# Four more chunk pairs of the FFNs in Strassen's form, a third set of partial-sum copies, and new written-out orders, in a four-layer linear-attention and SwiGLU kernel on one core

## The chip, the cores and the metric

The kernel runs on one core of one Trainium2 chip. The metric is the device time of one execution in microseconds. TensorE is called PE, VectorE DVE, ScalarE ACT, GpSimd POOL, and SyncE SP (here it only issues DMAs); PEld is PE's loading of weights.

## The reference

Four layers work on x, 2048 tokens by 512, in bfloat16. Layers 0 and 2 are linear attention, layers 1 and 3 are SwiGLU FFNs, each behind a layer norm and with a residual:

```python
def _A_ref(x, wqkv, wo):      # 32 heads of 16
    phi = lambda t: jnp.where(t > 0, t + 1, jnp.exp(t)) + 1e-6
    ...
    kv = jnp.einsum("bhsd,bhse->bhde", pk, v)
    num = jnp.einsum("bhqd,bhde->bhqe", pq, kv)
    ...
    return (o, heads side by side) @ wo
def _B_ref(x, w_gate, w_up, w_down):   # 512 -> 1792 -> 512
    return (_silu(x @ w_gate) * (x @ w_up)) @ w_down
x = x + _A_ref(_layernorm(x), ...)
x = x + _B_ref(_layernorm(x), ...)
x = x + _A_ref(_layernorm(x), ...)
x = x + _B_ref(_layernorm(x), ...)
```

## The kernel before, in words

Everything stays in SBUF. The 2048 tokens are 16 tiles of 128 (`T`), in 4 groups of 512 (`G`). The hidden width 1792 is 14 chunks of 128 (`NF`), taken as 7 pairs of chunks j and j+7 (`NK`).

**The order of the work is written out.** PE follows the list `PROGRAM`, one token per piece of work. A token is a layer, a letter and indices: `2k3` projects the keys of tile 3 in layer 2, `q` the queries, `g` adds a tile to the products of keys and normed rows, `v` and `m` make the four blocks of M (the merged key-value and output matrix, kept in `GT`), `w` multiplies a tile of queries by M and adds the residual, `u` is one gate-and-up chunk, `y` one Strassen product, `p` one Strassen product of the down projection. The other four engines follow the lists in `ORDER`, one name per instruction, as `1u104.h`. The program derives the semaphores from what each instruction reads and writes; an engine works through its list in order and waits at its head. PSUM has 8 banks; `bank()` gives the one whose last use stands longest ago in `PROGRAM`, so a matmul can wait for whoever reads that bank's last contents.

**A plain pair** (`gu`) is two `u` tokens: 16 matmuls of 512 columns (line 483, the one line of all matmuls but the transposes). For each chunk ACT takes the silu of the gate (L954, name `.silu`) and DVE multiplies by the up part (L959, `.h`). In layer 1, once layer 2 has begun, the silu is made of a tanh (`.tanh`, L942) and one more DVE pass (`.gst`).

**A Strassen pair** (`gs`) makes the same two chunks with 7 products instead of 8, each for gate and up at once: tokens `y` g j 1 to 7, 4 matmuls of 256 columns each, 28 in all. It needs sums of weight blocks (`gs_piece`, L1040, `.ws`), made for two pairs at a time, and of blocks of the transposed rows (`gs_rows`, L1086, four `.xs` per group of tokens). Products 1, 6, 7 and 4 add up in one PSUM bank, 5 and 3 in another, 2 has its own. After products 1, 6 and 7 ACT copies the running sum to SBUF (L1179, `.cp`). DVE adds such a copy to another bank (L1158, `.ca`) three times; ACT takes the silu of half of it (L1150, `.sih`, four times, once straight from PSUM); the gate-up product is one 256-column multiplication on POOL or DVE (L1173, `.hp`, three times) and one on DVE (L1189, `.hh`). The copies live in lent buffers (`gs_copies`): a set of three per pair in work. Two sets exist in layer 1, so two pairs can be open at once; layer 3 has a third set (`fam_slot`). 22 of the 56 pairs are in Strassen's form: three in layer 1 (group 1, j = 2, 0, 1) and 19 in layer 3.

**The down projection** (`down`, tokens `p`) is in Strassen's form everywhere, 14 matmuls of 256 columns per product. It needs sums of the hidden blocks (`sums_of_h`, L1251, `.sb` and `.sa`) and of blocks of w_down (`load_down`, L579, `Wd.tw`).

When the last Strassen pair that uses `Wo` as its home for row sums is through, `Wo` is read again from memory (`reload`, name `R.ldo`, a DMA that POOL issues, line 526). In `wo` (L905 to 912) the four matmuls of a tile take the blocks c = 0, 1, 2, 3 of M in this order, whatever order the `m` tokens have (`2m1 2m0 2m3 2m2` in layer 2, `0m0 0m2 0m1 0m3` in layer 0); `evac` (L786 on ACT, L789 on DVE) copies each block from PSUM to `GT`. `scale` (L882, `.pqn`) multiplies queries by 1/den and must come before the `w` of that tile.

Of the kernel before, what the change touches and what calls it, by code (L numbers as in the profile page):

```python
# [224 lines left out]
0q10.id1 0d0.rex2 i.c1 0q20.exp 0d1.ln 0d1.rex1 0d1.rex3 0G2.evac 0G3.evac 0q30.exp 0d1.rex2 0d1.rex 0q31.exp 0M0.evac
0M1.evac 0M3.evac 0q33.exp 0d2.ln 0d2.rxs 0q33.id1 1x1.sq 1x2.sq 1x3.sq 1x2.apply 1x0.sq 1x3.apply 0q32.exp 1x5.sq
1x6.sq 1x4.sq 1x11.sq 1u012.silu 1u001.silu 1x7.sq 1u007.silu 1x9.sq 1x4.apply 0d3.rep 1u000.silu 1u011.silu
1u006.silu 1u004.silu 0d3.rep1 1x7.apply 0d3.rep2 1u005.silu 1x6.apply 1u013.silu 1x10.sq 1u003.silu 1x8.sq 1u002.silu
0d3.rep3 1u010.silu 1u008.silu 1y121.cp 1x9.apply 1u113.silu 1u110.silu 1u009.silu 1u104.silu 1y101.cp 1y126.cp
# [1279 lines left out]
```

## Time and profile before

| what | value |
|---|---|
| median of 3 runs | 405.15 us (404.96 to 405.56) |
| profiled execution, its own time | 405.13 us |
| its span | 403.4 us |
| instructions | 7572 |
| PE, PEld, DVE, ACT, POOL busy | 397.1, 252.0, 331.8, 254.6, 176.8 us |
| granted clock of PE | 1.00 over the span |
| DMA | 23.84 MB, 59 GB/s mean |

The span runs from the first to the last instruction of the profile; some 1.7 us of the time lie around it. A PE matmul's bar in the profile is longer than the distance to the next one, as matmuls overlap; the distance between starts is what a matmul costs in a stream.

### The profile page before, as it was taken

The numbers are of one execution on the slowest core, as the hardware profiler recorded it, in microseconds if no ns is written. First come the engines' busy times: TensorE is split into PE (matmuls) and PEld (weight loads), VectorE is DVE, ScalarE is ACT, GpSimd is POOL, SyncE is SP. The second block draws the span as 40 slices with busy tenths as digits, with TensorE's granted clock in tenths as the row PEclk, the third lists the DMA queues.
The fourth block names the chain that finished last, engine by engine and source line by source line (L and its number), as shares of the span: only waits on it lengthen the run. The fifth ranks groups of instructions, "written<-read, shape, count | busy, mean of one in ns | idle before, by whom it ended". The sixth has DMA issues, their size and how long they took to land.

```text
span 403.4 us, 7572 instructions
## 1 busy us (share of the span) xinstructions
PE 397.1 (98%) x2798; PEld 252.0 (62%) x2798; DVE 331.8 (82%) x786; ACT 254.6 (63%) x525; POOL 176.8 (44%) x304
## 2 busy tenths in 40 slices
PE   7999999999999999999999999999999999999997
PEld 5445544445785764445776444444568788888886
DVE  5996598569986766979998476979889799899997
ACT  5999887483635537445166878686654673786550
POOL 4723335999787400210136603475677141421230
PEclk9999999999999999999999999999999999999999
DMA  8647682732002140010002105333200110100011
GB/s 273 157 80 238 154 160 63 191 72 28 2 13 67 26 80 13 2 39 0 2 16 52 39 3 78 66 54 78 41 13 2 41 53 2 53 2 2 2 52 54
DMA packets 53334, 23.84 MB, mean 59 GB/s; under 512 B 46448, under 2 KB 52080, under 8 KB 53296
## 3 DMA queue, kind: packets, MB, share of 16 engines
q1 hardware_dynamic: 51264, 16.27, 19.4%
q0 software_dynamic: 1488, 6.55, 5.1%
q10 hardware_dynamic: 544, 0.52, 0.4%
q8 instruction: 22, 0.36, 0.4%
q14 instruction: 16, 0.13, 0.1%
HBM read 10.22 MB, written 2.10 MB: 31 GB/s over the span
## 4 chain that ended last, share of the span: by engine, by line
PE 95%; DVE 2%; DMA 1%; issue 0%; SPq 0%; ACT 0%; DVEq 0%
PE pb L483 94%; DMA X<-in_A_x_dram 1%; DVE hT L959 0%; DVE X L912 0%; SPq L526 0%; ACT GT L786 0%; DVE Wd L579 0%; DVE xnB L646 0%; DVE pq L1371 0%; PE pb L670 0%; DVE pq L882 0%; DVE stats L600 0%; DVE xnA L1297 0%; DVE KVT L800 0%; DVEq L1479 0%
## 5 line engine op out<-in xcount | busy, mean ns | idle before, releaser
L483 PE MATMUL pb<-xnT,Wg 128*128 128x512 bf16 (+1 forms) x360 | 86.6, 353 | 0.1
L483 PE MATMUL pb<-xnT,Wu 128*128 128x512 bf16 (+1 forms) x360 | 86.6, 353 | 0.0
L483 PEld LDWEIGHTS pb<-xnT,Wu 128*128 128x128 bf16 x360 | 35.2, 98 | 33.1
L483 PEld LDWEIGHTS pb<-xnT,Wg 128*128 128x128 bf16 x360 | 35.1, 98 | 29.4 <-issue 0.6
L635 POOL TENSOR_TENSOR rstd<-vpe,negh 128x1 f32<-128x1 f32 x62 | 36.8, 595 | 19.3 <-DVE vpe L631 17.6
L959 DVE TENSOR_TENSOR hT<-tht,pb 128x512 bf16<-128x512 f32 x46 | 30.6, 681 | 16.6 <-ACT tht L954 10.2
L1179 ACT ACTIVATE pq<-pb 128x512 f32<-128x512 f32 x48 | 28.1, 595 | 24.4 <-PE pb L483 23.0
L954 ACT ACTIVATE tht<-pb 128x512 f32<-128x512 f32 x46 | 26.5, 591 | 23.4 <-PE pb L483 21.4
L1173 POOL TENSOR_TENSOR hT<-pq 128x256 bf16<-128x256 f32 x30 | 22.6, 762 | 42.3 <-ACT pq L1150 42.0
L483 PE MATMUL pb<-Wd,hT 128*128 128x256 bf16 x336 | 40.3, 273 | 0.0
L691 ACT ACTIVATE etmp<-pb 128x512 bf16<-128x512 f32 x64 | 36.3, 602 | 5.9 <-PE pb L483 3.7
L483 PEld LDWEIGHTS pb<-Wd,hT 128*128 128x128 bf16 x336 | 32.9, 98 | 4.9 <-POOL nmr L639 0.3
L1158 DVE TENSOR_TENSOR pq<-pb,pq 128x512 f32<-128x512 f32 x48 | 31.9, 684 | 4.1 <-PE pb L483 2.2
L483 PE MATMUL pb<-xnT,Wqkv 128*128 128x512 bf16 x128 | 32.2, 379 | 0.0
L696 DVE TENSOR_SCALAR etmp<-etmp 128x512 bf16<-128x512 bf16 x64 | 19.0, 304 | 15.2 <-ACT etmp L691 15.0
L483 PE MATMUL pb<-Wqkv,xnT 128*128 128x512 bf16 x128 | 31.2, 379 | 0.0
L483 PE MATMUL pb<-pk,xnA 128*128 128x512 bf16 x128 | 30.7, 379 | 0.0
L483 PE MATMUL pb<-GT,pq 128*128 128x512 bf16 x128 | 30.0, 379 | 0.4 <-ACT GT L786 0.3
L942 ACT ACTIVATE tht<-pb 128x512 f32<-128x512 f32 x22 | 12.8, 596 | 23.4 <-PE pb L483 20.3
L619 POOL TENSOR_SCALAR mv<-sums 128x1 f32<-128x1 f32 x52 | 13.5, 266 | 31.3 <-DVE sums L1381 22.0
L615 ACT ACTIVATE etmp<-X,sums 128x512 bf16<-128x512 bf16 x32 | 22.9, 717 | 5.7 <-DVE X L912 5.7
L1150 ACT ACTIVATE pq<-pq 128x256 f32<-128x256 f32 x48 | 18.8, 411 | 10.7 <-DVE pq L1158 10.4
(207 smaller groups left out, 837.8 us busy)
## 6 DMA issues: line engine op xcount, KB each, us to landing
out_dram<-pq SPq DMA_DIRECT2D x16, 128.0 KB, 1.8
Wg<-in_B_w_gate_dram POOLq DMA_DIRECT2D x4, 448.0 KB, 5.3
Wu<-in_B_w_up_dram POOLq DMA_DIRECT2D x4, 448.0 KB, 5.5
Wd<-in_B_w_down_dram POOLq DMA_DIRECT2D x7, 256.0 KB, 3.6
...
```

What stands on the lines that cost most here:

```text
L483: return op("pe", lambda e: e.matmul(o_ap, lhsT=lhsT, rhs=rhs, start=start, stop=stop, skip_group_check=skip), r=r, w=w, n=n)
L615: op("act", lambda a: a.activation(out=sq_ap, in_=X[:, t, :], func=ACT.Square, scale=-float(D), bias=sums[:, t:t + 1], accum_out=mv[:, t, ...
L619: op("pool", lambda p: p.tensor_scalar(out=mv[:, t, 0:1], in0=sums[:, t:t + 1], scalar1=-1.0 / D, scalar2=None, op0=ALU.mult), r=[f"sm{t}" ...
L635: op("pool", lambda p: p.tensor_tensor(out=rstd[:, t:t + 1], in0=vpe[:, t:t + 1], in1=negh[:], op=ALU.pow), r=[f"vp{t}", "negh"], w=[f"rs{ ...
L691: exps.append(op("act", lambda a: a.activation(out=etmp[e][:], in_=PB[pb], func=ACT.Exp), r=[f"pb{pb}"], w=[f"e{e}"], after=silus, kind="e ...
L696: op("dve", lambda v: v.tensor_scalar(out=etmp[e][:], in0=etmp[e][:], scalar1=1.0, scalar2=1e-6, op0=ALU.min, op1=ALU.add), r=[f"e{e}"], w ...
L954: silus.append(op("act", lambda e: e.activation(out=tht[a][:], in_=PB[pg], func=ACT.Silu), r=[f"pb{pg}"], w=[f"th{a}"], after=exps, kind=" ...
L959: op("dve", lambda v: v.tensor_tensor(out=hT[h][:, j, :], in0=tht[a][:], in1=PB[pu], op=ALU.mult), r=[f"pb{pu}", f"th{a}"], w=hk, kind="h")
L1150: silus.append(op("act", lambda e: e.activation(out=o_ap, in_=i_ap, func=ACT.Silu), r=r, w=w, after=exps, kind="sih" if len(w) == 1 else " ...
L1158: op("dve", lambda v: v.tensor_tensor(out=c, in0=PB[b], in1=c, op=ALU.add), r=[f"pb{b}", k], w=[k], kind="ca")
L1173: lambda e: e.tensor_tensor(out=hT[h][:, jj, o:o + 256], in0=c[:, 0:256], in1=c[:, 256:512], op=ALU.mult),
L1179: op("act", lambda e: e.activation(out=c, in_=PB[pb], func=ACT.Copy), r=pk_, w=[k], kind="cp")
```

## The change

- Layer 1: the pairs `1y13` (group 1), `1y21` and `1y20` (group 2) go into Strassen's form in place of `1u103 1u110`, `1u201 1u208` and `1u200 1u207`. Layer 3: `3y15` in place of `3u105 3u112`. The weight sums that they need are among those already made; group 2 of layer 1 needs its four row sums (`1gx2`, on POOL).
- Layer 1 gets a third set of copies too, in `GT` and `rrep`.
- Two plain chunks of layer 1, `1u209` and `1u211`, have their up part copied by ACT (`.uc`) and multiplied by POOL (`.hc`) instead of DVE's `.h`.
- `wo` takes the blocks of M in the order in which the `m` tokens stand.
- In the head, DVE makes the statistics of tile 2 (ACT did), and some tiny steps change places between POOL, DVE and ACT; `0g0` moves ahead of `0q03`.
- The lists of all engines are written anew around it. `KVT` becomes a part of `etmp`'s buffer.

```diff
@@ PROGRAM
-1u007 1u000 1u004 1u011 1u006 1u005 1u003 1u013 1u010 1u002 1y121 1u008 1u113 1u009 0w13 1u110 0w14 1y126 1y101 1u104
...
-1y122 1u105 1y106 0w15 1y125 1y102 0w12 1y127 1y107 1p01 1y124 1y123 1y105 1y104 1u112 1y103 1p05 1u103 1p06 1y111
+1u007 1u000 1u004 1u011 1u006 1u005 1u003 1u013 1u010 1u002 1y121 1u008 1u113 1u009 0w13 0w14 1y126 1y101 1u104 1y122
+1u105 1y106 0w15 1y125 1y102 0w12 1y127 1y107 1p01 1y131 1y124 1y132 1y136 1y123 1y105 1y137 1y104 1u112 1y135 1y134
+1y103 1p05 1p06 1y111 1y112 1y115 1p07 1y116 1p02 1y133 1y117 1p04 1p03 1y114 1u111 1y113 1u106 1u213 1u206 1y201 1p11
+1y211 1p15 1y216 1y206 1y212 1y217 1p16 1y215 1u210 1y213 1y214 1y202 1y207 1y205 1p17 1p12 1y204 1y203 1p14 1u203
...
+3y136 3y122 3y127 3y137 3p03 3y151 3y124 3y135 3y152 3y156 3u113 3y157 3y123 3y155 3p04 3y133 3y141 3y154 3y134 3y211
...
@@ ORDER, DVE
-1x11.apply Wd.tw8 1u002.h 1u010.h 0d3.pqn 1u008.h 0d3.pqn1 Wd.tw1 0d3.pqn2 0d3.pqn3 1u113.h 1u009.h 0w13.res 1u110.h
...
+0d3.pqn1 1u005.h 1u013.h 1u010.h 1x11.apply 0d3.pqn2 Wd.tw8 Wd.tw1 1u002.h 0d3.pqn3 1u008.h 0d3.pqn 1u113.h Wd.tw7
...
@@ ORDER, POOL
-1x13.vpe 1y122.hp Wd.tw3 1y123.hp 1y103.hp Wd.tw1 1y127.hp 1x8.pow 1x14.pow 1y105.hp 2x2.negm R.ldo 1x13.pow 1y112.hp
...
+1y122.hp Wd.tw5 1x14.pow 1x12.negm 1y123.hp 1y127.hp 1x14.nmr 1x13.pow 1x8.pow 1x15.vpe 1x13.negm 1x15.negm 1y112.hp
+1y103.hp R.ldo 1y133.hp 1y105.hp 1gx2.xs 1y135.hp 1x13.nmr 1y102.hp 1y117.hp 2x3.negm 1y113.hp 1y132.hp 1gx2.xs2
...
@@ m_mm, wo
+            m_of.setdefault(L, []).append(c)
...
-            for c in range(NC):
-                mm(pb, pq[n][:, c, tl * P:(tl + 1) * P], GT[:, c, :], c == 0, c == NC - 1,
+            for c in m_of[L]:
+                mm(pb, pq[n][:, c, tl * P:(tl + 1) * P], GT[:, c, :], c == m_of[L][0], c == m_of[L][-1],
@@ fam_slot
-            if L == 3 and r.left.get(r.k % 2, 0) > 0 and not third[0]:
+            if r.left.get(r.k % 2, 0) > 0 and not third[0]:
                 third[0] = True
+                if L == 1 and len(gs_tmp[L]) == 6:
...
+                    for x, olds in ((gt[:, 0:1024], ["GT0", "GT1"]), (gt[:, 1024:], ["GT2", "GT3"]), (rreps, ["rrep0", "rrep1"])):
...
                 return 2
```

## Rows read from the trace of the kernel before

**Rows 1.** The page: busy time by engine, and the ending chain's shares by engine

```profile
PE 397.1 (98%) x2798; PEld 252.0 (62%) x2798; DVE 331.8 (82%) x786; ACT 254.6 (63%) x525; POOL 176.8 (44%) x304
...
PE 95%; DVE 2%; DMA 1%; issue 0%; SPq 0%; ACT 0%; DVEq 0%
```

**Rows 2.** Timeline of PE, 101 to 107 us: start, us, what, out<-in, count

```profile
101.03 1.03 PE L483 MATMUL pb<-GT,pq 128*128 128x512 bf16 x4
101.89 0.60 PE L483 MATMUL pb<-Wo,xnA 128*128 128x256 bf16 x4
...
104.50 1.69 PE L483 MATMUL pb<-Wd,hT 128*128 128x256 bf16 x14
106.03 0.38 PE L483 MATMUL pb<-Wo,Wg 128*128 128x256 bf16 x2
```

**Rows 3.** The ending chain in order of time: start, us, what

```profile
91.97 0.35 DVE pq L882
...
262.57 1.94 DVE X L912 x6
```

**Rows 4.** Stretches: PE, PEld, DVE, ACT, POOL busy, clock, DMA

```profile
86.00:104.00 18.00, 17.86 (x99) 9.46 (x98) 17.92 (x29) 7.99 (x15) 17.86 (x19) 1.00 0.18 28
104.00:126.00 22.00, 22.00 (x179) 17.27 (x177) 19.37 (x53) 11.14 (x28) 16.13 (x21) 1.00 0.06 13
...
300.00:330.00 30.00, 30.00 (x262) 25.30 (x260) 26.66 (x53) 18.63 (x42) 14.31 (x19) 1.00 0.13 32
...
360.00:400.00 40.00, 39.95 (x367) 35.23 (x365) 38.89 (x80) 20.32 (x49) 7.87 (x11) 1.00 0.06 18
```

**Rows 5.** The page's costliest groups: busy, mean ns of one, idle before

```profile
L483 PEld LDWEIGHTS pb<-xnT,Wu 128*128 128x128 bf16 x360 | 35.2, 98 | 33.1
...
L959 DVE TENSOR_TENSOR hT<-tht,pb 128x512 bf16<-128x512 f32 x46 | 30.6, 681 | 16.6 <-ACT tht L954 10.2
L1179 ACT ACTIVATE pq<-pb 128x512 f32<-128x512 f32 x48 | 28.1, 595 | 24.4 <-PE pb L483 23.0
...
L1173 POOL TENSOR_TENSOR hT<-pq 128x256 bf16<-128x256 f32 x30 | 22.6, 762 | 42.3 <-ACT pq L1150 42.0
...
L1158 DVE TENSOR_TENSOR pq<-pb,pq 128x512 f32<-128x512 f32 x48 | 31.9, 684 | 4.1 <-PE pb L483 2.2
...
L1150 ACT ACTIVATE pq<-pq 128x256 f32<-128x256 f32 x48 | 18.8, 411 | 10.7 <-DVE pq L1158 10.4
```

**Rows 6.** Groups of instructions on POOL, 86 to 150 us, shapes apart

```profile
L1086 POOL TENSOR_TENSOR Wo<-xnT 128x512 bf16<-128x512 bf16 x2 | 2.5, 1272 | 0.0
```

**Rows 7.** Timeline of PE, 90 to 98 us

```profile
91.20 1.03 PE L483 MATMUL pb<-xnT,Wu 128*128 128x512 bf16 x4
92.37 1.04 PE L483 MATMUL pb<-GT,pq 128*128 128x512 bf16 x4
```

**Rows 8.** Timeline of DVE, 82 to 106 us

```profile
84.93 0.69 DVE L959 TENSOR_TENSOR hT<-tht,pb 128x512 bf16<-128x512 f32 x1 [1.69 <-ACT tht L954]
...
90.08 1.29 DVE L882 TENSOR_TENSOR pq<-pq,RT 128x512 bf16<-128x512 bf16 x1
...
91.90 0.41 DVE L882 TENSOR_TENSOR pq<-pq,RT 128x512 bf16<-128x512 bf16 x1
```

**Rows 9.** Timeline of POOL, 123 to 131 us

```profile
124.78 0.84 POOL L526 DMA_DIRECT2D Wo<-in_A_wo_dram  x1
...
126.19 2.08 POOL L1173 TENSOR_TENSOR hT<-pq 128x256 bf16<-128x256 f32 x3
```

**Rows 10.** Timeline of PE, 122 to 131.5 us

```profile
130.80 0.93 PE L483 MATMUL pb<-Wd,hT 128*128 128x256 bf16 x7
```

**Rows 11.** Timeline of all engines, 250 to 253 us

```profile
250.59 1.57 ACT L786 ACTIVATE GT<-pb 128x512 bf16<-128x512 f32 x3
...
251.81 1.46 PE L483 MATMUL pb<-GT,pq 128*128 128x512 bf16 x6 [0.28 <-ACT GT L786]
```

**Rows 12.** Timeline of all engines, 4 to 10 us

```profile
6.29 0.69 DVE L600 BATCH_NORM_STATS2 stats<-X 128x6 f32<-128x512 bf16 x1 [0.16 <-DMA X<-in_A_x_dram]
```

More of the change, by code (lines that the diff above doesn't have):

```diff
@@ L225 @@
[L225 to L229, printed above, removed]
@@ L267 @@
-0q23.ts 0q23.phi 0z.zm 0q22.ts 0q21.ts 0q10.ts 0q21.phi 0q22.phi 0q10.phi 0d0.pqn1 0q20.ts 0q20.phi 0G0.evac 0G1.evac
-0q30.ts 0v.mask 0v.mask1 0q30.phi 0d0.pqn 0q31.ts 0M2.evac 0q31.phi 0d1.pqn1 0q33.ts 0w1.res 0d2.dT 0w2.res 0q33.phi
-1x1.vpe 0w3.res 1x2.vpe 1x1.apply 0w0.res 0r2.pqn 0d1.pqn 1x3.vpe 0d1.pqn2 0r2.pqn1 0d1.pqn3 0r2.pqn2 1x0.vpe 0r2.pqn3
-0q32.ts 1x0.apply 0w5.res 0q32.phi 0w6.res 0w4.res 0w7.res 0w11.res 0d3.den 1x5.vpe 0w9.res 0w10.res 0w8.res 0d3.rcp
-1x5.apply 1u007.h 1u012.h 1u001.h Wd.tw 1x9.vpe 1x7.vpe 1u011.h 1u000.h 1u006.h 1u004.h 1u005.h 1u003.h Wd.tw6 1u013.h
@@ L292 @@
-2q23.phi 2q22.phi 2d0.pqn1 2G0.evac 2G1.evac 2d0.pqn 2v.mask 2v.mask1 2q33.ts 2d1.dT 2M3.evac 2r1.pqn 2r1.pqn1 2w3.res
-2r1.pqn2 2w2.res 2r1.pqn3 3x3.apply 2q33.phi 2w0.res 3x2.apply 2d2.pqn 2w1.res 2w4.res 2d2.pqn3 2d2.pqn2 3x1.vpe
-2q30.ts 2q30.phi 2d2.pqn1 2q32.ts 3x1.apply 2q32.phi 2w6.res 2w9.res 2w7.res 2w8.res 2w5.res 2w10.res 2d3.den 2d3.rcp
-3W1.ws2 2w11.res 3u001.h 3u004.h 3W1.ws4 3x4.apply 3x7.apply 3W1.ws 3u008.h 3W1.ws1 3u010.h 2d3.pqn 3x9.vpe 3u000.h
-3x9.apply 2w12.res 3W0.ws1 3W1.ws3 3W0.ws 2d3.pqn3 3x11.vpe 3u009.h 3x8.apply 3u005.h 3W2.ws 2d3.pqn1 2d3.pqn2
@@ new lines @@
+0G1.evac 0q30.ts 0v.mask 0v.mask1 0q30.phi 0M2.evac 0q31.ts 0d0.pqn 0q31.phi 0d1.pqn1 0q33.ts 0w1.res 0d2.dT 0w2.res
+0q33.phi 1x1.vpe 0w3.res 1x2.vpe 1x1.apply 0w0.res 0d1.pqn 1x3.vpe 0r2.pqn 0d1.pqn2 0r2.pqn1 0d1.pqn3 0r2.pqn2 1x0.vpe
+0r2.pqn3 0q32.ts 1x0.apply 0w5.res 0q32.phi 0w6.res 0w4.res 0w11.res 0d3.den 0w7.res 0w9.res 0w10.res 0w8.res 1x5.vpe
+1x9.vpe 1x5.apply 0d3.rcp 1u012.h 1u001.h 1u007.h 1u011.h 1x7.vpe 1u000.h 1u004.h 1u006.h Wd.tw 1u003.h Wd.tw6
+0d3.pqn1 1u005.h 1u013.h 1u010.h 1x11.apply 0d3.pqn2 Wd.tw8 Wd.tw1 1u002.h 0d3.pqn3 1u008.h 0d3.pqn 1u113.h Wd.tw7
@@ new lines @@
+2x8.apply 1p33.rh1 1p37.uu 2k11.ts 2k11.phi 1p37.rh 1p37.rh1 1p34.rh 1p34.tot 1p34.rh1 2x14.tot 2x14.vpe 1p32.rh1
+2x12.tot 2x15.vpe 2x14.apply 2q02.ts 1p32.rh 1p32.tot 2q02.phi 2x15.apply 2q00.ts 2q00.phi 2q12.ts 2q12.phi 2x12.apply
+2k9.ts 2k9.phi 2k10.ts 2k10.phi 2k8.ts 2k14.ts 2k8.phi 2k14.phi 2k15.ts 2k15.phi 2q11.ts 2k14.zs 2k13.ts 2k13.phi
+2k12.ts 2q11.phi 2k12.phi 2k13.zs 2q31.ts 2k12.zs 2q31.phi 2q21.ts 2s.zh 2s.zl 2q20.ts 2q20.phi 2z.zm 2q03.ts 2q03.phi
+2q21.phi 2q13.ts 2q23.ts 2q13.phi 2d0.pqn 2q22.ts 2q23.phi 2q22.phi 2d0.pqn1 2G0.evac 2G1.evac 2v.mask 2v.mask1
@@ new lines @@
+2q33.ts 2d1.dT 2M3.evac 2r1.pqn 2r1.pqn1 2w3.res 2r1.pqn2 2w2.res 2r1.pqn3 3x3.apply 2q33.phi 2w0.res 3x2.apply
+2d2.pqn 2w1.res 2q30.ts 2q32.ts 2q30.phi 2d2.pqn3 3x1.vpe 2d2.pqn2 2w4.res 2d2.pqn1 3x1.apply 2q32.phi 2w6.res 2w8.res
+3W1.ws2 3W1.ws4 2w9.res 2d3.den 2w7.res 2w5.res 2w10.res 3W1.ws 2w11.res 2d3.rcp 3u001.h 3W2.ws 3u008.h 3x7.apply
+3x4.apply 3W1.ws3 3W1.ws1 3x9.vpe 2d3.pqn 3u004.h 3W0.ws1 3u010.h 2d3.pqn1 3x11.vpe 3u000.h 3x9.apply 3W0.ws 2d3.pqn3
+2w12.res 3u005.h 3u009.h 3x8.apply 3u012.h 2d3.pqn2 2w15.res 3u002.h 3W0.ws2 3u011.h 3gx1.xs 2w14.res 2w13.res
@@ L314 @@
+3p35.uu 3p36.uu 3h3.sa3 3p36.uu1 3p32.rh1 3p33.rh 3p33.rh1 3p37.uu 3p37.rh 3p34.rh 3p37.rh1 3p34.rh1
 """,
     "pool": """
[L316 to L319 removed]
@@ new lines @@
+0x15.vpe 0x13.pow 0x14.nmr 0x15.pow i.c3 0x8.pow 0x12.vpe 0x12.pow i.ld i.ld3 i.ld2 i.ld1 i.ld4 i.ld8 0d0.pqn1 i.ld6
+i.ld7 i.ld5 0d0.pqn 1x1.negm 1x2.negm 1x1.pow 1x2.pow 1x2.nmr 1x3.pow 1x3.negm 1x0.negm 1x3.nmr 1x0.pow 1x4.negm
+1x6.negm 1x7.negm 1x4.vpe 1x5.negm Wd.ld2 1x4.pow 1x6.vpe 1x6.pow 1x5.pow 1x11.negm 1x6.nmr Wd.ld 1x4.nmr Wd.ld1
+1x11.vpe 1W0.ws4 1x9.pow Wd.ld4 1W0.ws6 1W1.ws Wd.ld5 1x7.pow 1x11.pow 1x7.nmr Wd.ld3 Wd.ld6 1W1.ws1 1W0.ws5 1W1.ws2
+1x9.negm 1W0.ws 1W1.ws4 1x9.nmr 1W1.ws5 1x8.negm 1W1.ws6 Wd.tw6 1gx1.xs 1x10.vpe 1x10.pow 1gx1.xs1 1W1.ws7 1W0.ws1
@@ L933, in gu @@
             hk = [f"h{h}_{j}a", f"h{h}_{j}b"]
-            uc = rreps[:, 0:1024].bitcast(FP32) if L == 1 and f"1c{g}{j:02d}" in ON_ACT else None
+            late = f"{L}c{g}{j:02d}" in ON_ACT and ("rrep0" not in pr.lent if L == 1 else all(f"2w{t}" in given for t in range(T)))
+            uc, uk = (rreps[:, 0:1024].bitcast(FP32), ["rrep0", "rrep1"]) if L == 1 else (etmps[:, 1024:2048].bitcast(FP32), ["uc"])
+            if late and L == 3 and "uc" not in pr.bufs:
+                lend(L, "uc", ["e2", "KVT0", "KVT1"])
+                take_over(L)
             def half(scale):
                 op("act", lambda e: e.activation(out=uc, in_=PB[pu], func=ACT.Copy, scale=scale),
-                   r=[f"pb{pu}"], w=["rrep0", "rrep1"], kind="uc")
+                   r=[f"pb{pu}"], w=uk, kind="uc")
                 op("pool", lambda e: e.tensor_tensor(out=hT[h][:, j, :], in0=tht[a][:], in1=uc, op=ALU.mult),
-                   r=["rrep0", "rrep1", f"th{a}"], w=hk, kind="hc")
+                   r=uk + [f"th{a}"], w=hk, kind="hc")
             if L == 1 and any(x[1] in "kq" and x[0] == "2" for x in given):
@@ L946, in gu @@
                    r=[f"pb{pg}", f"th{a}"], w=[f"th{a}"], kind="gst")
-                if uc is not None:
+                if late:
                     half(0.5)
@@ L955, in gu @@
                                 r=[f"pb{pg}"], w=[f"th{a}"], after=exps, kind="silu"))
-                if uc is not None:
+                if late:
                     half(1.0)
```

265 lines of the change are left out of this document (134 added, 131 removed).

## The prediction

> **What bounds the kernel now.** I read the page first: PE is busy 98% of the span, and 95% of the chain that ended last runs through it [rows 1]. Since matmul bars overlap, a full bar alone shows no full PE; so next I read the distance between starts in PE's timeline. Four matmuls of 512 columns take 101.89 - 101.03 = 0.86 us, 215 ns each; the 14 of 256 columns from 104.50 take 106.03 - 104.50 = 1.53 us, 109 ns each [rows 2]. That is the same time per column, in a stretch of Strassen work. The chain in order of time then shows how little is left: it leaves PE only where PE waits, and apart from the first 8 us and the last 4 these breaks are short, as the one that ends with a DVE step at 91.97 and the one behind six residual steps at 262.57 [rows 3]. So PE's matmul time is the bound, and any other gain must come out of one of these few waits. The stretches show who stands next in line: DVE, with 17.92 of 18 us busy from 86 to 104, beside POOL with 17.86, and again 38.89 of 40 us from 360 to 400 [rows 4].
>
> **The change part by part.**
>
> *Four pairs in Strassen's form.* A plain pair is 16 x 215 ns = 3.44 us of PE, a Strassen pair 28 x 109 ns = 3.06 us [rows 2]. Four pairs: 4 x 0.38 = **-1.52 us**, all on the path.
>
> What PE saves the others pay. ACT: three copies of 595 ns and four silus of 411 ns, 3.43 us, for two silus of about a copy's length (same shape, also from PSUM), 1.19 us [rows 5]: +2.2 us a pair. DVE: three adds of 684 ns and one half-width product (0.34 to 0.68 us, half and all of a plain `.h`; I take the middle, 0.5), 2.55 us, for two `.h` of 681 ns [rows 5]: +1.2 us. POOL: three products of 762 ns [rows 5], +2.3 us. Group 2 of layer 1 adds four `.xs` on POOL at 1272 ns, 5.1 us [rows 6]. None of this is on the path as long as it finishes before its reader: ACT works 11.14 of 22 us from 104 to 126, and POOL 16.13 [rows 4], so both have room; where the cover is thin I work it out below. The third set of copies adds no instruction; it lets pair 13 open while 12 and 10 are open.
>
> *`1u209` and `1u211`.* Two `.h` of 0.68 us leave DVE; ACT gets two copies of 0.6 us; POOL two products that this trace doesn't have, between one `.hp` of 762 ns and two of them, 1.5 us [rows 5], and I take 1.5 as they have twice the columns. Their reader, the down products of group 2, stands some ten tokens behind. Nothing on the path; if POOL were late, up to 1.5 us.
>
> *The wait at 92.37.* Four matmuls that start at 91.20 are through at 92.06, yet the first `w` of the group starts at 92.37 [rows 7]: 0.31 us. It waits for `0d3.pqn1`, which DVE reaches only behind `Wd.tw8`, three `.h` and a `.pqn` [rows 3]. The new list puts `Wd.tw6` and `0d3.pqn1` ahead of `1u005.h`, where DVE stood idle for 1.69 us before its next `.h` [rows 8]. **-0.31** (0 to -0.31). Next in line is `0w14`, whose `.pqn2` moves ahead too.
>
> *A thinner cover behind it.* `1u110` went, eight matmuls or 1.72 us of PE, while DVE got only 0.68 us lighter, and DVE was full there [rows 4]. PE now comes 2.0 us earlier to `1y102`. Its bank is the one that `1u104.h` reads last, and that stands behind `1u105.h` in the new list; `1u105` ends at about 98.6, two `.h` later it is 100.1, and PE arrives at 100.3. `1y123` waits for `1y127.ca`, which needs the full DVE queue to be on time. The idle time that the moved steps use about pays for it. **+0.1** (0 to +0.9).
>
> *R.ldo ahead of the products.* `R.ldo` overwrites the row sums in `Wo`, so it waits for `1y114`, the last reader. It used to stand with most products of group 1 in front of it and three right behind it [rows 9]; now `1y133.hp`, `1y105.hp`, `1gx2.xs`, `1y135.hp`, `1y102.hp`, `1y117.hp`, `1y113.hp` and `1y132.hp` and two tiny steps queue behind it. `1p11` started at 130.80 [rows 10]. Ahead of it there are now pair 13 and `1y201` (+3.06 + 0.44), but not `1u110`, `1u103` (-3.44) and the wait (-0.31): 130.55, and its fourth matmul, the first that needs pair 13's product, at 130.9. Four `u` and two `y` tokens (7.8 us) stand between, so `1y114` ends at 122.8. POOL needs from 123.0: 0.84 for the issue [rows 9], seven products at 0.69 from start to start (2.08 us for three, [rows 9]), one `.xs` of 1.27 [rows 6], two tiny steps of 0.3: 7.5 us, so 130.5 to 130.9. **+0.1** (0 to +2.7, rival B).
>
> *The order of M's blocks.* In layer 2 ACT copies three blocks in 1.57 us, 0.49 apart: block 1 is there at 251.2, block 0 at 251.7. PE's first `w` starts with block 0 and waits until 251.81 [rows 11]. With block 1 first it can start about 0.4 us sooner, but then its second matmul waits for block 0: the gain is one matmul, 0.215 us. Some of it is lost at 264.5, where PE waits for DVE's residual steps [rows 3], which don't come sooner, as the new list puts two weight sums among them. **-0.1** (0 to -0.22). In layer 0 I see no wait of PE at this place: nothing.
>
> *The head.* Tile 2's statistics go to DVE (0.69 + 0.18) and delay tile 0's apply by 0.7 us. But tile 0 is copied out only behind the statistics of tile 1, whose data land at 6.29 [rows 12], and that doesn't change. **0** (-0.1 to +0.3). `0g0` ahead of `0q03`: the same matmuls, nothing. `KVT` in `etmp`'s buffer: the same bytes, nothing. SP issues the same 112 DMAs, some neighbours in another order: nothing.
>
> *Layer 3's new pair* adds 1.2 us to DVE where it is busy 26.66 of 30 us, 300 to 330 [rows 4]. With the two plain chunks gone, PE comes up to 3.4 us sooner to `3y104`, which needs sums from POOL; those the new POOL list moves ahead of `3gx2`'s. **0** (0 to +1.6, rival A).
>
> Sum: -1.52 - 0.31 + 0.10 + 0.10 - 0.10 = -1.73 us on a profiled 405.13, which is 0.02 below the median: 405.15 - 1.73 = **403.4 us**.
>
> **A rule against it.** The rows say that a 256-column matmul costs 109 ns in a stream, with a weight load of 98 ns beside it [rows 2, 5], so the load is hidden, by 11 ns. The Trainium skill, "TensorE: Matmul & The Clock Gate", section "Back-to-back issue gap", says that in streams of loads and matmuls both set the spacing, and gives 81 ns at 128 columns and 131 ns at 512. By that a narrow matmul costs more per column and each new pair would lose; the trace does not agree (109 against 215). What it would make of the sum is worked out from the rows as rival C.
>
> **The rivals.**
>
> A, *the gain is given back by DVE*. For it: 38.89 of 40 us busy before the end, 26.66 of 30 before that [rows 4]. If DVE is the true pace there, the pair in layer 3 costs DVE's 1.2 us in place of giving 0.38: 403.4 + 1.58 = 405.0. Against it: PE streams at full rate through these stretches.
>
> B, *slower: POOL late behind `R.ldo`*. If its queue takes 1.4 times as long, 10.6 us in place of 7.5, `1y132.hp` ends at 133.6 and `1p11` waits 2.7 us for it: 403.4 - 0.1 + 2.7 = 406.0. It costs from 7.9 us on, and makes the kernel slower than before from 9.8. For it: DVE and POOL work stretches each other's steps; the same `.pqn` took 1.29 and 0.41 us [rows 8] in the full stretch. Against it: the three products in that place came at 0.69 us apart [rows 9]. The Trainium skill, "SBUF — State Buffer", section "Who interferes with whom", says that DVE and POOL hold their shared ports by turns for a whole instruction; the stretched `.pqn` agrees.
>
> C, *narrow matmuls pay for their loads*. If half of a 98 ns load showed, a matmul would cost 158 ns and a pair 4.42: +0.98 in place of -0.38, 4 x 1.36 more than forecast, 408.8. Against it [rows 2].
>
> That the change does not do what it says: the new pairs could share nothing and need more weight sums. The code excludes it, as pairs 0 to 3 take pieces 0 and 1, which exist.
>
> **How the numbers follow.** 0.2% is 0.81 us, about what a measurement of this kernel can tell. Forecast 0.75; A 0.13; B 0.10; C 0.02. The forecast is faster by 1.73; A is within the bound; B and C are slower. So faster 0.75, same 0.13, slower 0.12. Low end: all gains at their bounds, and an estimated 0.4 for other short waits, as the rest of that at 251.81 (0.28 idle, [rows 11]): 405.15 - 1.52 - 0.31 - 0.22 - 0.1 - 0.4 = 402.6. The high end takes in A and the +0.9 of the thin cover in part, 405.2; B and C stay out.
>
> **What would show it.** PE's matmuls rise from 2798 to 2846, and 26 pairs keep 109 ns. The chain loses its break at 92; the wait before the first `w` of layer 2 shrinks to one matmul behind the first. A wait for POOL before `1p11` shows B; waits for DVE past 300 us show A; starts 150 ns apart in the Strassen stretches show C. I am wrong if PE has new waits of over 0.9 us in all, as that leaves less than 0.81 of the gain.

## The result and the profile after

The changed kernel takes **410.43 us** (median of 4 runs, 409.46 to 412.4), the kernel before, on the same chip, 405.05 (404.67 to 405.56): a ratio of 1.0138, 95% interval 1.0099 to 1.0177. It was forecast 1.7 us faster and is 5.4 us slower. Line numbers are each kernel's own from here on.

The page of the changed kernel, beside [rows 1]:

```profile
PE 398.1 (97%) x2846; PEld 256.5 (62%) x2846; DVE 344.1 (84%) x792; ACT 261.4 (64%) x545; POOL 190.9 (46%) x321
...
PE 81%; DVE 9%; DMA 3%; ACT 3%; POOL 2%; issue 1%; SPq 0%; DVEq 0%; POOLq 0%; ACTq 0%
```

The 48 more matmuls are there, and the chain now leaves PE for a fifth of the span instead of a twentieth. DVE has six steps more than before but is busy 12.3 us longer. What PE waited for from 15 us on, in all, how often, and the longest time:

```profile
PE pb L488 <- DVE rT L861: 2.1, 1, 2.1
PE pb L488 <- DVE hT L971: 2.0, 1, 2.0
PE pb L488 <- DVE X L1391: 1.7, 1, 1.7
PE pb L488 <- DVE X L920: 0.8, 1, 0.8
PE pb L488 <- DVE vpe L636: 0.6, 1, 0.6
PE pb L488 <- ACT tht L966: 0.4, 1, 0.4
PE pb L488 <- DVE etmp L805: 0.2, 1, 0.2
```

Seven single waits, all but one for DVE, and none ahead of `1p11` or past 300 us, where rivals B and A put theirs. The second and the third matter most. The timelines of PE, DVE and POOL around the second:

```profile
88.44 1.03 PE L488 MATMUL pb<-xnT,Wg 128*128 128x512 bf16 x4
91.51 0.82 PE L488 MATMUL pb<-xnT,Wu 128*128 128x512 bf16 x3 [2.04 <-DVE hT L971]
...
86.92 2.64 DVE L584 TENSOR_TENSOR Td<-Wd 128x256 bf16<-128x256 bf16 x1 [0.98 <-DMA Wd<-in_B_w_down_dram]
89.49 1.36 DVE L890 TENSOR_TENSOR pq<-pq,RT 128x512 bf16<-128x512 bf16 x1
90.78 1.27 DVE L971 TENSOR_TENSOR hT<-tht,pb 128x512 bf16<-128x512 f32 x2
...
86.92 1.15 POOL L1052 TENSOR_TENSOR xnA<-Wg 128x512 bf16<-128x512 bf16 x1
88.05 0.25 POOL L624 TENSOR_SCALAR mv<-sums 128x1 f32<-128x1 f32 x1
88.27 1.14 POOL L1052 TENSOR_TENSOR pk<-Wg 128x512 bf16<-128x512 bf16 x1
89.37 1.20 POOL L1052 TENSOR_TENSOR xnA<-Wu 128x512 bf16<-128x512 bf16 x1
```

DVE's rows are `Wd.tw6`, `0d3.pqn1` and, as one, `1u005.h` and `1u013.h`. The up matmuls at 91.51 need the bank that `1u005.h` reads. DVE first stood 0.98 us until data of `Wd` had landed; then the two predecessors of `1u005.h` took 2.64 and 1.36 us, while POOL went from one sum of weights straight to the next. The same around the third, at `1p03.tot`, the smallest kind of step there is:

```profile
135.31 0.39 PE L488 MATMUL pb<-xnT,Wu 128*128 128x512 bf16 x1 [1.67 <-DVE X L1391]
...
131.70 3.21 DVE L1401 TENSOR_TENSOR sums<-sums,sumr 128x1 f32<-128x1 f32 x1
134.83 0.41 DVE L1391 SCALAR_TENSOR_TENSOR X<-pb,pq 128x256 bf16<-128x256 f32 x1
...
131.44 1.16 POOL L1098 TENSOR_TENSOR pk<-xnT 128x512 bf16<-128x512 bf16 x1
132.55 0.72 POOL L1193 TENSOR_TENSOR hT<-rrep 128x256 bf16<-128x256 f32 x1
133.27 0.25 POOL L644 TENSOR_SCALAR nmr<-mv,rstd 128x1 f32<-128x1 f32 x1
133.50 1.39 POOL L1193 TENSOR_TENSOR hT<-pq 128x256 bf16<-128x256 f32 x2
```

128 additions lasted 3.21 us, until 134.91; POOL's string ended at 134.89. `1p03.rh1` behind it reads the bank that PE wants.

The first wait, for `rT`, stands in the profiled execution, which was the longest of the four. PE stood still, and in the 3.5 us behind that its granted clock was 0.52, about half: the lower of its two levels (1.2 GHz). The stretches (us, busy time of PE, PEld, DVE, ACT, POOL, granted clock, DMA):

```profile
56.00:59.00 3.00, 0.86 (x19) 0.33 (x17) 1.75 (x6) 0.47 (x1) 0.24 (x1) 0.99 0.74 98
59.00:62.50 3.50, 3.50 (x27) 1.29 (x15) 3.48 (x14) 3.05 (x8) 2.31 (x6) 0.52 0.13 27
```

The other three executions have a mean clock of 1.000, and are 1.8 to 2.9 us shorter.

### The profile page after: what moved, and what is told of

The parts are those of the page before. It is cut to its first block, busy times and chain, and to the rows that moved or that the text cites. A ratio compares the mean times of both kernels' runs of the same rounds, so it can differ in the third digit from the quotient of the medians.

```text
span 410.7 us, 7718 instructions
## 1 busy us (share of the span) xinstructions
PE 398.1 (97%) x2846; PEld 256.5 (62%) x2846; DVE 344.1 (84%) x792; ACT 261.4 (64%) x545; POOL 190.9 (46%) x321
## 4 chain that ended last, share of the span: by engine, by line
PE 81%; DVE 9%; DMA 3%; ACT 3%; POOL 2%; issue 1%; SPq 0%; DVEq 0%; POOLq 0%; ACTq 0%
PE pb L488 81%; DMA RT<-rrep 2%; DVE X L920 2%; DVE pq L908 1%; DMA X<-in_A_x_dram 1%; DVE pq L890 1%; DVE sums L1401 1%; DVE RT L1271 1%; DVE hT L971 1%; POOL rstd L640 1%; ACT tht L966 1%; ACT etmp L696 1%; ACT pq L699 0%; ACT rrep L871 0%; DVE xnB L651 0%
## 5 line engine op out<-in xcount | busy, mean ns | idle before, releaser
L488 PE MATMUL pb<-xnT,Wu 128*128 128x512 bf16 (+1 forms) x344 | 81.4, 347 | 3.7 <-DVE hT L971 2.0
L488 PE MATMUL pb<-xnT,Wg 128*128 128x512 bf16 (+1 forms) x344 | 81.4, 347 | 1.2 <-DVE X L920 0.8
L488 PEld LDWEIGHTS pb<-xnT,Wu 128*128 128x128 bf16 x344 | 33.5, 98 | 33.7 <-DVE hT L971 2.7
L488 PEld LDWEIGHTS pb<-xnT,Wg 128*128 128x128 bf16 x344 | 33.3, 98 | 28.4 <-DVE dsb L856 1.3
L1199 ACT ACTIVATE pq<-pb 128x512 f32<-128x512 f32 x54 | 31.5, 595 | 27.1 <-PE pb L488 22.3
L1193 POOL TENSOR_TENSOR hT<-pq 128x256 bf16<-128x256 f32 x36 | 26.5, 746 | 43.9 <-ACT pq L1170 43.7
L1178 DVE TENSOR_TENSOR pq<-pb,pq 128x512 f32<-128x512 f32 x54 | 36.2, 683 | 5.1 <-PE pb L488 4.6
L966 ACT ACTIVATE tht<-pb 128x512 f32<-128x512 f32 x40 | 23.2, 593 | 26.5 <-PE pb L488 16.6
L971 DVE TENSOR_TENSOR hT<-tht,pb 128x512 bf16<-128x512 f32 x40 | 26.7, 681 | 12.1 <-ACT tht L966 7.3
L1170 ACT ACTIVATE pq<-pq 128x256 f32<-128x256 f32 x54 | 21.3, 411 | 5.5 <-DVE pq L1178 5.4
L954 ACT ACTIVATE tht<-pb 128x512 f32<-128x512 f32 x20 | 11.8, 601 | 15.6 <-PE pb L488 15.5
```

What stands on the lines that cost most here:

```text
L488: return op("pe", lambda e: e.matmul(o_ap, lhsT=lhsT, rhs=rhs, start=start, stop=stop, skip_group_check=skip), r=r, w=w, n=n)
L966: silus.append(op("act", lambda e: e.activation(out=tht[a][:], in_=PB[pg], func=ACT.Silu), r=[f"pb{pg}"], w=[f"th{a}"], after=exps, kind=" ...
L971: op("dve", lambda v: v.tensor_tensor(out=hT[h][:, j, :], in0=tht[a][:], in1=PB[pu], op=ALU.mult), r=[f"pb{pu}", f"th{a}"], w=hk, kind="h")
L1170: silus.append(op("act", lambda e: e.activation(out=o_ap, in_=i_ap, func=ACT.Silu), r=r, w=w, after=exps, kind="sih" if len(w) == 1 else " ...
L1178: op("dve", lambda v: v.tensor_tensor(out=c, in0=PB[b], in1=c, op=ALU.add), r=[f"pb{b}", k], w=[k], kind="ca")
L1193: lambda e: e.tensor_tensor(out=hT[h][:, jj, o:o + 256], in0=c[:, 0:256], in1=c[:, 256:512], op=ALU.mult),
```

## The experiments

A kernel that takes the changed order for one layer alone has everything else as before, but for the home of `KVT`, which is the new one in all of them. The diffs show stretches of the lists, not whole lines. Times are medians; a ratio is to the kernel before, on the same chip. Not all runs were on one chip, so a difference of two medians can differ from that of the two ratios by some 0.5 us; where it matters both are given.

### The head alone

```diff
@@ ORDER, POOL
-i.ld6 i.ld7 0d0.pqn 1x1.negm i.ld5
+i.ld6 i.ld7 i.ld5 0d0.pqn 1x1.negm
@@ ORDER, DVE
-0w11.res 0d3.den 1x5.vpe 0w9.res 0w10.res 0w8.res
+0w11.res 0d3.den 0w7.res 0w9.res 0w10.res 0w8.res 1x5.vpe
```

> Layer 0 in the changed order (with the 448 KB weight load i.ld5 ahead of 0d0.pqn on POOL's queue), everything from layer 1 on, the pairs by Strassen's form and the order of M among it, as before. Theory (the new place of i.ld5 makes the transposing DMAs of 0d1 land late, which no later stage gives back): a wait of 1.5 to 2.5 us for DVE ahead of 0r2 near 56 us, none of that size anywhere else, and 406 to 407.5 us in all, since the new start of the head gives back about 0.6. Rival (layer 1's lists are the whole cause, and the lateness of the head is absorbed by the slack behind it): 404.3 to 405.2 us.

408.03 us, ratio 1.0065 [1.0044, 1.0085]. The head does cost, 2.9 us (2.6 by the ratio) and more than I thought, but not where I said: PE waits for `.h` steps of layer 1 at 87.80 and 92.12, and not ahead of `0r2`. The profiled execution is one of the shorter ones (407.04).

### `i.ld5` back in its place

```diff
@@ ORDER, POOL
-i.ld6 i.ld7 i.ld5 0d0.pqn 1x1.negm
+i.ld6 i.ld7 0d0.pqn 1x1.negm i.ld5
```

> The changed kernel whole, but POOL's weight load i.ld5 stands behind 1x1.negm again, as before the change. Theory: 0d1's transposes land some 4 us sooner, the wait of 2.3 us ahead of 0r2 shrinks to under 0.5, and the time falls by 1.5 to 2.5 us to 407.5 to 409 us; the waits near 89 and 133 us stay. Rival (the load's place is no cause of the late transposes, or layer 1's waits grow by what the head gives back): 410 to 410.8 us.

410.51 us (409.73 to 412.32), as the changed kernel: my theory falls. The wait for `rT` is gone from its profile, but so it is from that of e_after_dve below, which has `i.ld5` in the changed place; that wait belonged to one execution, and the load's place is no cause. With `i.ld5` back, one of the five executions (412.32) has a mean clock of 0.996 too, as the profiled one of the changed kernel.

### Layer 1 alone, layer 3 alone, the order of M alone

```diff
@@ ORDER, DVE (layer 1)
-1u004.h 1u005.h 1u003.h Wd.tw6 1u013.h
+1u003.h Wd.tw6 0d3.pqn1 1u005.h 1u013.h
@@ ORDER, POOL (layer 1)
-1y105.hp 2x2.negm R.ldo 1x13.pow 1y112.hp
+1y103.hp R.ldo 1y133.hp 1y105.hp 1gx2.xs 1y135.hp 1x13.nmr 1y102.hp 1y117.hp
```

> Layer 1 alone in the changed order, with its two more chunk pairs by Strassen's form and the third set of copies; layer 0, layers 2 and 3 and the order of M as before. Theory (layer 1's lists make waits of their own: DVE has Wd.tw6 and 0d3.pqn1 ahead of 1u005.h, and small DVE steps such as 1p03.tot stand behind POOL's string of copies): waits of 1.5 to 2.5 us near 89 to 91 us and near 133 us, 407 to 409 us. Rival (those waits were only the late head, handed on): no wait over 0.7 us in layer 1, and 404 to 404.8 us, the two pairs' gain of 0.76 us on TensorE kept.

407.28 us, 1.0051 [1.0033, 1.0068]. Layer 1 gets three pairs more, not two, so on PE they save 1.14 us and not 0.76. The wait at 1p03's bank is there with all of its size (1.67 us), without any late head; the one for `1u005.h` is not. So the first is layer 1's own, and the second needs both. `Wd.tw6` and `0d3.pqn1` in its timeline of DVE, in the same order as in the changed kernel:

```profile
82.52 0.36 DVE L580 TENSOR_TENSOR Td<-Wd 128x256 bf16<-128x256 bf16 x1 [0.32 <-DMA Wd<-in_B_w_down_dram]
82.80 1.56 DVE L886 TENSOR_TENSOR pq<-pq,RT 128x512 bf16<-128x512 bf16 x1
```

Together 1.9 us in place of 4.0, behind an idle time of 0.32 in place of 0.98. PE also waits 0.81 us for a residual step ahead of `3u001` here, where layer 3's order is that of before.

```diff
@@ ORDER, DVE (layer 3)
-2w6.res 2w9.res 2w7.res 2w8.res 2w5.res 2w10.res 2d3.den
+2w6.res 2w8.res 3W1.ws2 3W1.ws4 2w9.res 2d3.den 2w7.res 2w5.res 2w10.res 3W1.ws
```

> Layer 3's feed-forward stage alone in the changed order, with its two more pairs by Strassen's form; layers 0 to 2 and the order of M as before. Theory (the pairs there do save what the fewer matmuls save, 0.76 us, less some 0.3 of the two inserted combinations of weights between layer 2's residuals): 404.4 to 405.0 us, and a wait of 0.5 to 1 us ahead of 3u001. Rival (VectorE paces layer 3 as well and takes the gain back, or more): 405.2 to 406.5 us, with waits for DVE past 300 us.

404.67 us, 0.9986 [0.9976, 0.9996]: a gain in the expected range, and no wait for DVE past 300 us. But layer 3 gets one pair more (0.38 us), not two, and the wait expected ahead of `3u001` is not in its profile.

```diff
@@ wo
-            for c in range(NC):
+            for c in m_of[L]:
```

> The kernel before with one part of the change alone: the output rows take the blocks of M in the order in which they are made. Theory: the wait of 0.44 us ahead of the first output rows of layer 2 shrinks to some 0.2 us, and 404.8 to 405.1 us in all. Rival (the products behind it wait for the same GT copies, so that nothing moves): 405.1 us.

405.00 us, 0.9992 [0.9983, 1.0001]; the size fits the theory, but the interval holds no change too. The four parts multiply to 1.0094, the whole change is 1.0138: some 1.8 us are left for where the late head meets layer 1's order. The five intervals together leave about 2 us of doubt on that; what speaks for it is the wait of 2.04 us near 89 us, which neither part has alone.

### Why the head costs: one step of 0.15 us

```diff
@@ ORDER, DVE (on e_head_only)
-0w7.res 0w9.res 0w10.res 0w8.res 1x5.vpe
+0w7.res 1x5.vpe 0w9.res 0w10.res 0w8.res
```

> e_head_only with one step moved: on DVE 1x5.vpe stands ahead of 0w9.res again, as before the change, and no longer behind the three residual additions 0w9, 0w10 and 0w8. Theory (POOL takes its steps in order and stands at 1x5.pow until 1x5.vpe is done, 1.9 us later than before; the copies, ACT's steps behind 1x7.nmr and with them 1u005.h on DVE are late by the same 1.9 us, and TensorE waits 0.5 and 1.1 us at 87 and 91 us): 1x5.pow starts near 67.3, those two waits fall under 0.2 us, and the time falls from 408.0 to 405 to 406.5 us. Rival (the head's loss is elsewhere: in its DMAs or in the 57 to 62 us stretch): 407.5 to 408.5 us.

405.63 us, 1.0019 [1.0008, 1.0031]: 2.4 of 2.9 us are back (by the ratios 1.9 of 2.6). In the kernel before, `1x5.pow` stands so in POOL's timeline:

```profile
67.23 0.57 POOL L635 TENSOR_TENSOR rstd<-vpe,negh 128x1 f32<-128x1 f32 x1
```

The timelines of DVE and POOL of e_head_only, with `1x5.vpe` and `1x5.pow`:

```profile
68.91 0.15 DVE L629 TENSOR_SCALAR vpe<-mv 128x1 f32<-128x1 f32 x1
...
66.60 0.19 POOL L629 TENSOR_SCALAR vpe<-mv 128x1 f32<-128x1 f32 x1
69.14 0.57 POOL L633 TENSOR_TENSOR rstd<-vpe,negh 128x1 f32<-128x1 f32 x1 [2.35 <-DVE vpe L629]
```

Then those of e_head_vpe:

```profile
67.54 0.15 DVE L629 TENSOR_SCALAR vpe<-mv 128x1 f32<-128x1 f32 x1
...
67.77 0.57 POOL L633 TENSOR_TENSOR rstd<-vpe,negh 128x1 f32<-128x1 f32 x1 [0.52 <-DVE vpe L629]
```

POOL stood for 2.35 us at a step that waits for 0.15 us of DVE work behind three residual additions. Its whole queue came 1.9 us late, with it ACT's `1x7.apply` (80.70 before, 82.60 here), the silus behind that, and DVE's `1u005.h` (82.55 and 84.45); PE noticed some 19 us later, by waits of 0.34 and 0.92 us at 87.80 and 92.12, both gone now.

### Why `1p03.tot` lasts: POOL's string

```diff
@@ ORDER, POOL (on e_l1_only)
-1y105.hp 1gx2.xs 1y135.hp 1x13.nmr 1y102.hp 1y117.hp 2x3.negm
+1y105.hp 1y135.hp 1x13.nmr 1y102.hp 1y117.hp 2x3.negm 1gx2.xs
```

> e_l1_only with one step of POOL moved: 1gx2.xs, 1.16 us, from ahead of 1y135.hp to behind 2x3.negm, that is out of the string of POOL steps during which DVE's 128x1 step 1p03.tot lasts 3.22 us; DVE's order is untouched. Theory (a DVE step on two operands in SBUF gets no turn while POOL goes from one step straight to the next): 1p03.tot ends when the shorter string ends, so it takes 1.9 to 2.3 us, the wait ahead of the second half of 1u111's successor falls from 1.83 to 0.5 to 0.9 us, and the time falls by about 1 us to 406 to 406.6 us. Rival (1p03.tot waits for a result of its own, and POOL has nothing to do with it): 3.2 us again, and 407 to 407.6 us.

406.41 us, 1.0035 [1.0024, 1.0045]; PE's wait went from 1.7 to 0.6 us. A new one of 0.26 us, for POOL, stands at 132.20, ahead of the fourth matmul of `1p11`: rival B's place. The timelines of DVE and POOL in e_l1_only:

```profile
125.86 3.22 DVE L1397 TENSOR_TENSOR sums<-sums,sumr 128x1 f32<-128x1 f32 x1
...
125.60 1.16 POOL L1094 TENSOR_TENSOR pk<-xnT 128x512 bf16<-128x512 bf16 x1
126.71 0.73 POOL L1189 TENSOR_TENSOR hT<-rrep 128x256 bf16<-128x256 f32 x1
127.43 0.26 POOL L640 TENSOR_SCALAR nmr<-mv,rstd 128x1 f32<-128x1 f32 x1
127.66 1.40 POOL L1189 TENSOR_TENSOR hT<-pq 128x256 bf16<-128x256 f32 x2
```

And in e_l1_xs_later:

```profile
125.83 2.11 DVE L1397 TENSOR_TENSOR sums<-sums,sumr 128x1 f32<-128x1 f32 x1
127.86 0.41 DVE L1387 SCALAR_TENSOR_TENSOR X<-pb,pq 128x256 bf16<-128x256 f32 x1
...
125.58 0.73 POOL L1189 TENSOR_TENSOR hT<-rrep 128x256 bf16<-128x256 f32 x1
126.29 0.25 POOL L640 TENSOR_SCALAR nmr<-mv,rstd 128x1 f32<-128x1 f32 x1
126.52 1.40 POOL L1189 TENSOR_TENSOR hT<-pq 128x256 bf16<-128x256 f32 x2
```

DVE's order is the same in both; POOL's string ends 1.14 us sooner, and the step is 1.11 us shorter. Each time it ends within 0.02 us of the string: 129.08 and 129.06, 127.94 and 127.92. It does not wait for a result of its own.

### The two waits moved on DVE: a half miss

```diff
@@ ORDER, DVE
-Wd.tw6 0d3.pqn1 1u005.h 1u013.h
+1u005.h Wd.tw6 0d3.pqn1 1u013.h
...
-1p03.tot 1p03.rh1 1u111.h 1y114.hh
+1u111.h 1p03.tot 1p03.rh1 1y114.hh
```

> The changed kernel whole, with two orders on DVE altered: 1u005.h ahead of Wd.tw6 and 0d3.pqn1, and 1p03.tot with 1p03.rh1 behind 1u111.h. Theory (these two places are where TensorE waits 2.2 and 1.8 us, because a long DVE step stands ahead of the one it waits for): the waits near 89 and 133 us fall under 0.6 us each, and the time falls by 2.5 to 4 us to 406.5 to 408 us. Rival (DVE has no room, the waits come back at the next step of DVE's queue): 409.5 to 410.5 us.

408.54 us, 1.0095 [1.0071, 1.0119]: 1.9 us, less than expected. The wait of 2.04 us near 89 us is gone (one of 0.9 for `hT` came 5 us later, behind a `1x11.apply` that lasted 3.31 us); the one at 1p03's bank stands at 1.7. Another, at `1y102`, is the thin cover of the prediction, where PE waits for `1u104.h`:

```profile
102.75 0.39 PE L488 MATMUL pb<-xnT,Wg 128*128 128x256 bf16 x2 [0.47 <-DVE hT L971]
```

I had taken `1u111.h` for the step that PE waited for; it is `1p03.rh1`.

The second of these edits alone, on the changed kernel with layer 0 in the order of before:

```diff
@@ ORDER, DVE
-1p03.tot 1p03.rh1 1u111.h 1y114.hh
+1u111.h 1p03.tot 1p03.rh1 1y114.hh
```

> The changed kernel with layer 0 in the order of before and with 1p03.tot and 1p03.rh1 behind 1u111.h on DVE. Theory (head 2.9 and layer 1's one wait 1.8 are most of the loss; the four pairs and the order of M keep their gain, less the 0.8 us wait at 1p17): 404 to 405.2 us. Rival (layer 1 as a whole loses by its order, whatever stands ahead of 1u111.h): 406 to 407.5 us.

405.97 us, 1.0025 [1.0014, 1.0035]: between the two forecasts, 0.03 us under the rival's. The step was moved, and PE's wait stayed at 1.67 us. The timelines of DVE and POOL in e_best1:

```profile
125.98 0.68 DVE L968 TENSOR_TENSOR hT<-tht,pb 128x512 bf16<-128x512 f32 x1
126.57 2.62 DVE L1398 TENSOR_TENSOR sums<-sums,sumr 128x1 f32<-128x1 f32 x1
...
127.78 1.39 POOL L1190 TENSOR_TENSOR hT<-pq 128x256 bf16<-128x256 f32 x2
```

Reached later, the step is held shorter, but to the same end, that of the string (129.19 and 129.17). `1u111.h` in front of it, which reads PSUM, took its usual 0.68 us beside the same string.

### Ahead of the string

```diff
@@ ORDER, DVE (on the changed kernel with layer 0 as before)
-1p03.rh 1p04.tot 1p04.rh1 1y117.ca 1y113.ca 1p03.tot 1p03.rh1 1u111.h
+1p03.rh 1p03.tot 1p03.rh1 1p04.tot 1p04.rh1 1y117.ca 1y113.ca 1u111.h
```

> The changed kernel with layer 0 in the order of before and with 1p03.tot and 1p03.rh1 right behind 1p03.rh on DVE, ahead of POOL's string. TensorE's wait of 1.83 us was for 1p03.rh1, which reads the bank that the next up product needs: behind 1u111.h the step still fell into the string and lasted 2.62 us. Theory: 1p03.tot takes 0.2 us, that wait falls under 0.3 us, and the time falls from 406.0 to 403.9 to 404.7 us, faster than the kernel before. Rival (the next reader of the string, 1u111.h or 1h1.sb, holds TensorE instead): 405.3 us or more.

404.27 us (403.55 to 404.93), **0.9971 [0.9961, 0.998]**: it beats the kernel before. `1p03.tot` in its timeline of DVE, and all that PE waits for from 15 us on:

```profile
123.37 0.16 DVE L1398 TENSOR_TENSOR sums<-sums,sumr 128x1 f32<-128x1 f32 x1
...
PE pb L485 <- DVE X L917: 0.9, 1, 0.9
PE pb L485 <- ACT GT L788: 0.2, 1, 0.2
PE pb L485 <- DVE etmp L802: 0.2, 1, 0.2
PE pb L485 <- issue: 0.2, 1, 0.2
```

PE has no wait left in layer 1, with its three pairs in it. The wait that remains, for a residual step, is the one at `3u001`. POOL's string is still there, and now it holds another step of DVE, `2x0.tot`, until 129.26, while the string ends at 129.24. The timelines of DVE and POOL:

```profile
127.41 1.85 DVE L1398 TENSOR_TENSOR sums<-sums,sumr 128x1 f32<-128x1 f32 x1
...
127.84 1.40 POOL L1190 TENSOR_TENSOR hT<-pq 128x256 bf16<-128x256 f32 x2
```

PE does not wait for that one.

```diff
@@ ORDER, DVE (on e_best2)
-2w8.res 3W1.ws2 3W1.ws4 2w9.res 2d3.den 2w7.res 2w5.res
+2w8.res 2w9.res 2w7.res 2w5.res 3W1.ws2 3W1.ws4 2d3.den
```

> e_best2 with three DVE steps, 3W1.ws2, 3W1.ws4 and 2d3.den (0.41, 0.41 and 0.28 us), moved from between layer 2's residual additions to behind 2w5.res. Theory (the one wait that e_best2 has left, 1.09 us ahead of 3u001, is for 2w7.res, which frees the bank and stands behind these inserted steps): the wait falls to 0.2 to 0.5 us and the time by 0.5 to 0.9 us, to 403.3 to 403.8 us. Rival (3u001 waits for the transposing DMA of 3x1, which the moved steps don't touch): 404.0 to 404.4 us.

404.72 us, 0.9993 [0.998, 1.0007]: a miss, and above the rival's range too; the move gained nothing over e_best2 (0.9971). The rival had the wait:

```profile
PE pb L485 <- DMA xnT<-xnB: 1.2, 1, 1.2
```

With the residual step out of the way PE waits for the transposing DMA of 3x1, as in e_best1 (0.77 us). Nor do the three steps between the residuals make the wait: e_l1_only has it (0.81 us) with none of them there, e_l3_only has them there and no such wait. Why the time rose by 0.45 us (0.9 by the ratios), with 0.25 us more of wait, stays open.

### All repairs in the changed kernel

```diff
@@ ORDER, DVE
-0w7.res 0w9.res 0w10.res 0w8.res 1x5.vpe
+0w7.res 1x5.vpe 0w9.res 0w10.res 0w8.res
...
-1u003.h Wd.tw6 0d3.pqn1 1u005.h 1u013.h 1u010.h 1x11.apply 0d3.pqn2 Wd.tw8 Wd.tw1 1u002.h
+1u003.h 1u005.h Wd.tw6 0d3.pqn1 1u013.h 1u010.h 1u002.h 1x11.apply 0d3.pqn2 Wd.tw8 Wd.tw1
...
-1p03.rh 1p04.tot 1p04.rh1 1y117.ca 1y113.ca 1p03.tot 1p03.rh1 1u111.h
+1p03.rh 1p03.tot 1p03.rh1 1p04.tot 1p04.rh1 1y117.ca 1y113.ca 1u111.h
@@ ORDER, ACT
-1x7.sq 1x4.apply 1u000.silu 0d3.rep 1u007.silu 1u001.silu
+1x7.sq 1u001.silu 1u007.silu 1x4.apply 1u000.silu 0d3.rep
```

> The changed kernel whole, with its orders on DVE and ACT altered at five places: 1x5.vpe ahead of 0w9.res; 1u005.h ahead of Wd.tw6; 1u002.h ahead of 1x11.apply; 1p03.tot and 1p03.rh1 right behind 1p03.rh, where POOL has a gap; on ACT 1u001.silu and 1u007.silu ahead of 1x4.apply. Theory (every microsecond that the change lost is a step that stands behind another engine's string or behind a long step on its own queue; with 1u005.h moved and 1p03.tot moved but still inside POOL's string it was 408.5): the waits near 75, 92 and 131 us, 0.56, 1.03 and 1.83 us there, fall under 0.4 us each, and the time falls to 404.8 to 406.2 us. Rival (the lists have no room left, each repair moves a wait to the next step): 407.5 us or more.

405.99 us (404.98 to 408.39), 1.0027 [1.001, 1.0045]: four changed places on DVE and one on ACT are worth 4.4 of the 5.4 us. The three waits named are gone. It is 1.7 us behind e_best2, which has the old head, and `1u005.h`, `1u002.h` and ACT's silus in the places of the changed kernel. Its executions spread over 3.4 us, those of e_best2 over 1.4. The profile, of one of the longest (408.14), has waits of 0.3 to 0.4 us for DVE between 58 and 65 us, one of 0.71 for POOL's row sums at 97.65 and one of 0.97 for the DMA of 3x1. Whether the 1.7 us come from the head alone, and why it spreads, was not settled.

## Why the prediction was wrong, point by point

The forecast was 403.4 us and the time 410.4, 7.0 us more. Three steps of it failed; undoing them is worth 2.4, 1.9 and 1.7 us, each in another kernel, so that the three need not add up. First, for rival C, eight matmuls of the new pairs of group 2 in PE's timeline of the changed kernel, and what starts next:

```profile
142.68 1.04 PE L488 MATMUL pb<-pk 128*128 128x256 bf16 x8
143.55 0.38 PE L488 MATMUL pb<-xnT,Wg 128*128 128x256 bf16 x2
```

- *Strassen's pairs, -1.52.* The mechanism held. The eight take 143.55 - 142.68 = 0.87 us, 109 ns each as forecast, which speaks against C. The kernel that has all four pairs, the old head and `1p03.tot` ahead of the string is 1.1 us faster than before (e_best2), although PE waits 0.9 us at `3u001` in it. The pairs alone, without new orders, were not run. Rival A fell: no wait for DVE past 300 us, and layer 3 alone gains (e_l3_only).
- *The wait at 92.37, -0.31.* **A step that failed.** It is gone, as forecast, but I took it that two more steps fit into DVE's idle 1.69 us [rows 8], where in the old order they had taken 0.79 and 0.41 us. (I misread the row, too: those 1.69 us end with `1u003.h` and stand behind `1u005.h`.) In their new place POOL's weight sums ran without a gap; with the late head DVE stood 0.98 us for data first, then they took 2.64 + 1.36 us; `1u005.h` behind them came late, and PE waited 2.04 us. Undoing that order is worth 1.9 us (e_after_dve, whose other edit left its wait as it was).
- *R.ldo ahead of the products, +0.1 (0 to +2.7).* **The second.** I worked out 7.5 us from `R.ldo` to the end of `1y132.hp`. That is what POOL needs when nothing holds it (123.54 to 131.02 in e_best2). I did not ask what the string does to DVE while it lasts: `1p03.tot` 3.21 us, PE 1.7 us. Nor what that does to POOL: in the changed kernel it stood 1.52 us for a sum of DVE behind `1p03.tot`, and the 7.5 us became 8.8, over the 7.9 from which rival B costs. `1p11` did not wait, as PE was itself 1.67 us late by then; e_l1_xs_later, where PE lost only 0.56, has 0.26 us of B's wait. Taking `1p03.tot` out of the string is worth 1.7 us (e_best1 against e_best2; 2.2 by the ratios). Rival B had the place and the sign, but another victim.
- *The head, 0 (-0.1 to +0.3).* **The third, and by the medians the largest.** I looked at the statistics of tile 2 and at bytes, and passed over `1x5.vpe`, which moved behind three residual additions: 2.4 of the 2.9 us that the head costs (e_head_vpe). The other 0.5 stay open.
- *Thinner cover, +0.1 (0 to +0.9); M's order, -0.1; layer 3's pair, 0; `1u209` and `1u211`, 0.* In the changed kernel no wait at `1y102` or `1y123`, but PE had been held up by 2.04 us before; with that undone, 0.47 us at `1y102`, inside the range (e_after_dve). -0.08% for M's order, an interval that holds no change too; layer 3 gains. POOL's two products took 1.28 and 1.39 us (1.5 forecast), and PE waits for none.
- *What would make it wrong* named new waits of over 0.9 us in all; the list above has 7.8 us, 2.1 of them in one execution only. The chance of 0.12 for slower rested on one place (B) and on C; the lists of five engines were written anew, and each moved step was such a place.
